# Half of a feed-forward layer's products rewritten as seven half-size products, with their sums shared out over three engines

## The chip, the cores and the metric

The kernel runs on one core of a Trainium2 chip. TensorE (PE in the profile) multiplies, VectorE (DVE) and ScalarE (ACT) read the results from PSUM, GpSimd (POOL) issues the loads and SyncE (SP) the stores and the DMA transposes. The metric is the device time of one execution in microseconds; the number compared is the median of several runs.

## What is computed

Chunked attention, then a feed-forward layer. `q`, `k`, `v` have the shape 8 x 8 heads x 576 x 64, in chunks of 64 tokens:

```
scores = 0.125 * (q_chunk @ k_chunk^T);  attn = softmax(scores);  out = attn @ v_chunk
x = out, heads side by side                # 4608 tokens x 512
h = x @ w_in                               # 512 x 2048
g = h / (1 + exp(-beta * h))
result = g @ w_out                         # 2048 x 512, float32
```

## The kernel before

**Blocks.** The 4608 tokens are nine blocks `j` of 512 tokens (two units of 256). While block `j` goes through the first layer, block `j-1` goes through the second, and the two units `2j+2` and `2j+3` go through attention. The kernel gives the order of all instructions itself: for each block a list `items` of (position in the block from 0 to 1, tie-break, work) is sorted, and the work is emitted in that order. Every engine runs its own instructions strictly in that order, each after its waits.

**First layer.** `emit_m(j, m)` makes 128 of the 2048 features for 512 tokens: four matmuls of 128x512 (`KDM` = 4 slices of the 512 inputs) into a PSUM bank `hps`, then ScalarE's tanh into `sg`, then VectorE's gate, `(sg + 1) * hps`, into the fp16 tile `gt`. Sixteen `m` make a block. `hps` comes from a pool `ps_p` of four PSUM banks.

**Second layer.** From block 1 on it is already made as seven products in place of eight (Winograd's form of Strassen's scheme): `emit_prod(j, p, t)`, eight matmuls of 128x256 for each of `p` in (1, 2, 6, 5, 7, 3, 4) and `t` in (0, 1). `emit_sum` makes the four sums `sm[0..3]` of `gt` on VectorE, `emit_wt` the four of `w_out` once. The products accumulate in two PSUM banks, `ya` (1, 6, 7, 4) and `yb` (2, then 5, 3). Partial results are copied out by ScalarE between the products, and VectorE adds the rest.

**Attention.** For unit `u` of the later blocks: `emit_T` (two DMA transposes on SP's queue, q and k), `emit_sc` (scores, then ScalarE's exponential into `et`), `emit_pv` for the halves s = 0 and 1, `emit_norm` (VectorE: a reciprocal and a product), `emit_xt_dma` (a DMA transpose on SP's queue into `xt`, which the next block's first layer reads). Scores and both halves of the PV product share one pair of PSUM banks, the pool `ps_s` with one buffer: each of the three waits until the one before it has been read. `loads_to` issues the loads of later units on GpSimd; it is called at the end of `emit_T`. The eight PSUM banks from block 3 on: four `ps_p`, two `ps_s`, `ya`, `yb`.

Of the kernel before, what the change touches and what calls it, by code (L numbers as in the profile page):

```python
# [8 lines left out]
FP32 = mybir.dt.float32  # L9
FP16 = mybir.dt.float16  # L10
ACTF = mybir.ActivationFunctionType
ALU = mybir.AluOpType
# [3 lines left out]
def kernel(  # L16
# [18 lines left out]
    NU = NT // UNIT  # L35
    NTILE = NT // 128
    VP = 80
    NV = 16
    HF = DFF // 2
    scale = 1.0 / float(D) ** 0.5  # L40

# [8 lines left out]
    gt_p = ctx.enter_context(tc.tile_pool(name="gt", bufs=2))  # L50
    sg_p = ctx.enter_context(tc.tile_pool(name="sg", bufs=3))
    osb_p = ctx.enter_context(tc.tile_pool(name="osb", bufs=4))
    osl_p = ctx.enter_context(tc.tile_pool(name="osl", bufs=6))
    ps_p = ctx.enter_context(tc.tile_pool(name="ps_p", bufs=4, space=bass.MemoryType.PSUM))
    ps_s = ctx.enter_context(tc.tile_pool(name="ps_s", bufs=1, space=bass.MemoryType.PSUM))
    ps_x_open = tc.tile_pool(name="ps_x", bufs=1, space=bass.MemoryType.PSUM)
    ps_x = ps_x_open.__enter__()
    ps_y = []

    ident = const.tile([128, 128], FP16)  # L60
    idle = const.tile([128, 512], FP16)
    HH = H // 2
    raw0 = [const.tile([128, HH, 2, D], FP32, name=f"raw{i}") for i in range(2)]
    qk0 = [[const.tile([128, HH, 2, D], FP16, name=f"h0{i}{a}") for i in range(2)] for a in range(2)]
    qkT0 = [[const.tile([128, HH, CH, 2], FP16, name=f"t0{i}{a}") for i in range(2)] for a in range(2)]
    braw = const.tile([128, 32], FP32)
# [3 lines left out]
    vbig = big.tile([128, NV, H, VP], FP16)  # L70
    wt = [big.tile([128, 8, 256], FP16, name=f"wt{i}") for i in range(4)]
    sm = [big.tile([128, 8, 256], FP16, name=f"sm{i}") for i in range(4)]

    blocks = [(u, 2) for u in range(0, NU, 2)]
    NB = len(blocks)
# [51 lines left out]
    def loads_to(u):  # L127
        while nxt[0] <= min(u, NU - 1):
            load_unit(nxt[0])
            nxt[0] += 1  # L130
# [16 lines left out]
    def emit_T(u, which=("kT", "qT")):  # L147
        for nm in which:
            src, dst = {"kT": (k_t, kT), "qT": (q_t, qT)}[nm]
            a = src.pop(u)  # L150
            t = qt_p.tile([128, H, CH, 2], FP16, tag=nm, name=nm)
            dst[u] = t
            if u >= XU:
                nc.sync.dma_start_transpose(
                    out=t.rearrange("p h s e -> p (h s e)").rearrange("p (j t) -> p j t", t=128),
                    in_=a.rearrange("p h r d -> p (h r d)"),
                )
                continue
            nc.vector.transpose(
                out=t.rearrange("p h s e -> p (h s e)").bitcast(FP32).rearrange(  # L160
                    "p (h i r) -> p h r i", h=H, r=2),
                in_=a.rearrange("p h r d -> p (h r d)").bitcast(FP32).rearrange(
                    "p (h r i) -> p h r i", h=H, r=2),
            )
        loads_to(u + 4)

    et_t = {}
    x_t = {}
# [104 lines left out]

    def emit_xt_pe(u, s):
        xf = x16_t.pop((u, s)).rearrange("p r h d -> p (r h d)")
        xp = ps_p.tile([128, 4, 128], FP16, tag="p", name="xp")
        xt = xt_at(u, s)
        for g in range(4):
            nc.tensor.transpose(out=xp[:, g, :], in_=xf[:, g * 128:(g + 1) * 128], identity=ident)  # L279
            if u == 0 and g % 2:  # L280
                nc.scalar.copy(out=xt[:, g - 1:g + 1], in_=xp[:, g - 1:g + 1])
        if u:
            nc.scalar.copy(out=xt, in_=xp)  # L283
# [4 lines left out]

    gt_t = {}

    def emit_m(j, m, c0=0, n=None):
        n = blocks[j][1] * UNIT if n is None else n
        if j not in gt_t:
            gt_t[j] = gt_p.tile([128, KFF, 512], FP16, tag="gt", name="gt")
        hps = ps_p.tile([128, 512], FP32, tag="p", name="hps")
        xr = xt_t[j].rearrange("p t (r k) (c q) -> p (t r) (k c) q", r=2, c=2)
        for kk in range(KDM):
            nc.tensor.matmul(  # L298
                out=hps[:, 0:n],
                lhsT=w_in16[m // 2][:, kk, (m % 2) * 128:(m % 2) * 128 + 128],  # L300
                rhs=xr[:, c0 // CH:(c0 + n) // CH, 2 * (kk % 2) + kk // 2, :],
                start=(kk == 0),
                stop=(kk == KDM - 1),
            )
        sg = sg_p.tile([128, 512], FP32, tag="sg", name="sg")
        nc.scalar.activation(out=sg[:, 0:n], in_=hps[:, 0:n], func=ACTF.Tanh, scale=bt[:, m:m + 1])  # L306
        nc.vector.scalar_tensor_tensor(  # L307
            out=gt_t[j][:, m, c0:c0 + n], in0=sg[:, 0:n], scalar=1.0, in1=hps[:, 0:n],
            op0=ALU.add, op1=ALU.mult,
        )  # L310
# [3 lines left out]
    def emit_t(j, t, k0=0, k1=None):  # L314
        k1 = KFF if k1 is None else k1
        if k0 == 0:
            ops_t[j, t] = ps_p.tile([128, DM], FP32, tag="p", name="ops")
        ops = ops_t[j, t]
        for kk in range(k0, k1):
            nc.tensor.matmul(  # L320
                out=ops,
                lhsT=gt_t[j][:, kk, t * 128:(t + 1) * 128],
                rhs=w_out16[kk // 4][:, kk % 4, :],
                start=(kk == 0),
                stop=(kk == KFF - 1),
            )
        if k1 < KFF:
            return
        osb = osb_p.tile([128, DM], FP32, tag="osb", name="osb")
        nc.scalar.copy(out=osb, in_=ops)  # L330
        r0 = blocks[j][0] * UNIT + t * 128
        nc.sync.dma_start(out=out[r0:r0 + 128, :], in_=osb)
# [19 lines left out]
    def emit_sum(j, i, lo=0, hi=8):  # L352
        g = gt_t[j]
        s1, s2 = sm[0][:, lo:hi, :], sm[1][:, lo:hi, :]
        a11, a12 = g[:, lo:hi, 0:256], g[:, 8 + lo:8 + hi, 0:256]
        a21, a22 = g[:, lo:hi, 256:512], g[:, 8 + lo:8 + hi, 256:512]
        a, b, op = ((a21, a22, ALU.add), (s1, a11, ALU.subtract),
                    (a11, a21, ALU.subtract), (a12, s2, ALU.subtract))[i]
        nc.vector.tensor_tensor(out=sm[i][:, lo:hi, :], in0=a, in1=b, op=op)  # L359

    acc_t = {}
    oq_t = {}
# [19 lines left out]
    def emit_prod(j, p, t):  # L382
        last = j == NB - 1
        if p == 1 and t == 0:
            if j == 1:
                a = [ps_p.tile([128, 512], FP32, tag="p", name="acc") for _ in range(2)]
            else:
                a = [ps_y[0].tile([128, 512], FP32, tag=n, name=n) for n in ("ya", "yb")]
            if last:
                a = [(a[i], ps_p.tile([128, 512], FP32, tag="p", name="acc")) for i in range(2)]  # L390
            acc_t[j] = a
        g = gt_t[j]
        acc = acc_t[j][0 if p in (1, 6, 7, 4) else 1]
# [33 lines left out]
                     7: (1, 1, "add"), 3: (0, 1, "add"), 4: (1, 0, "copy")}[p]  # L427
        key = (j, r, c, t if last else None)
        if how == "copy":
            o = osl_p.tile([128, 256], FP32, name="osl") if last else osb_p.tile([128, DM], FP32, tag="osb", name="osb")  # L430
            oq_t[key] = o
            nc.scalar.copy(out=o, in_=acc)  # L432
        else:
            o = oq_t[key]
            nc.vector.tensor_tensor(out=o, in0=acc, in1=o, op=ALU.add)
# [1 line left out]
            late.append(key)  # L437

    def emit_idle(n, w):
        d = ps_p.tile([128, 512], FP32, tag="p", name="warm")  # L440
        for _ in range(n):
            nc.tensor.matmul(out=d[:, 0:w], lhsT=idle[:, 0:128], rhs=idle[:, 0:w])

    with tc.manual_schedule():
# [93 lines left out]
        def att_items(u, a0, w):  # L538
            if u >= XU:
                return [(a0, 2, ("sc", u)), (a0 + 0.34 * w, 3, ("pv", u, 0)),  # L540
                        (a0 + 0.35 * w, 3, ("norm", u, 0)), (a0 + 0.60 * w, 3, ("pv", u, 1)),
                        (a0 + 0.61 * w, 3, ("norm", u, 1)), (a0 + 0.10 * w, 3, ("T", u + 1))]
            return [(a0, 2, ("sc", u)), (a0 + 0.40 * w, 3, ("pv", u)),
                    (a0 + 0.41 * w, 3, ("norm", u, 0)), (a0 + 0.55 * w, 3, ("norm", u, 1)),
                    (a0 + (0.70 if u + 1 < XU else 0.10) * w, 3, ("T", u + 1))]

        for j in range(1, NB):
            if j == 3:
                ps_x_open.__exit__(None, None, None)
                ps_y.append(ctx.enter_context(tc.tile_pool(name="ps_y", bufs=1, space=bass.MemoryType.PSUM)))  # L550
            items = []
            if j == 1:
# [3 lines left out]
                          (0.80, 3, ("norm", 4, 1)), (0.74, 3, ("Th", 5, "kT")), (0.86, 3, ("Th", 5, "qT"))]  # L556
            else:
                m0 = 0.36 if j == 2 else 0.02
                items += [(m0 + (1 - m0) * m / KFF, 0, ("m", m)) for m in range(KFF)]
                for i, p in enumerate((1, 2, 6, 5, 7, 3, 4)):  # L560
                    for t in range(2):
                        items.append((0.98 * (2 * i + t) / 14, 1, ("prod", p, t)))
                if j == NB - 1:
                    for i, c in ((2, 0.74), (0, 0.82), (1, 0.86), (3, 0.90)):
                        items.append((c, 4, ("pre", i)))
                for i in range(4):
                    s0 = (0.01, 0.08, 0.25, 0.33)[i] if j == 2 else 0.005 + 0.07 * i
# [12 lines left out]
            for _, _, it in items:  # L580
                if it[0] == "m":
                    emit_m(j, it[1])
                elif it[0] == "h":
                    emit_m(j, it[1], 256, 256)
                elif it[0] == "prod":
# [55 lines left out]
```

## Time and profile before

| quantity | value |
|---|---|
| median of three runs (lowest to highest) | 288.31 us (288.10 to 288.41) |
| the profiled execution's own time | 289.32 us |
| its span, first to last instruction | 287.5 us, granted TensorE clock 0.992 |
| PE / DVE / ACT / POOL busy | 95% / 68% / 51% / 34% of the span |
| blocks 3 to 7, first matmul to first matmul | 28.4 us each |
| block 8, and the second layer of block 8 with the last stores | 26.0 us and 15.8 us |

The profiled execution takes 1.0 us more than the median of the runs; 1.8 us of its time lie outside its span. "Busy" counts overlapping instructions of an engine once. In rows of instruction groups the form is given as output<-inputs (partitions x elements, type), then count, total busy us, mean ns of one, and the idle time of the engine ahead of it with what ended it.

### The profile page before, as it was taken

The page shows a single profiled execution, that of the slowest core. Times are in us where ns is not written, and L with a number is a line of the kernel's source. Part 1 is how long each engine was busy: PE and PEld are TensorE (multiplying, and loading weights), DVE is VectorE, ACT ScalarE, POOL GpSimd, SP SyncE. Part 2 cuts the span into 40 slices and gives each one's busy share as a digit, 9 for nine tenths or more (in the row PEclk, how much of TensorE's full clock was granted, in tenths as well). Part 3 has the DMA queues.
Part 4 walks back from the last instruction along what each step waited for, and adds up shares of the span by engine and source line. Part 5 has one row for each costly group of instructions (what it writes and reads, how often), then busy time and mean ns, then how long its engine had stood idle before and what let it go on. Part 6 is the DMA issues. An engine that isn't in the chain of part 4 may idle for free.

```text
span 287.5 us, 7407 instructions
## 1 busy us (share of the span) xinstructions
PE 272.6 (95%) x3090; PEld 175.7 (61%) x3090; DVE 195.6 (68%) x327; ACT 147.9 (51%) x235; POOL 97.0 (34%) x124
## 2 busy tenths in 40 slices
PE   7769999796999999999999999999999999999995
PEld 3555445653856566666666666666666666666684
DVE  3557538789577768576858685868576857685841
ACT  2368406884356464646463646364536454545521
POOL 8854578486474923434090707000000000000000
PEclk9999999999899999999999999999999999999999
DMA  9999999999999998999999998990748123110213
GB/s 138 171 196 204 174 172 187 232 167 130 109 98 150 141 214 118 149 130 193 119 105 161 178 145 105 129 228 18 112 96 144 22 55 95 53 39 31 70 48 109
DMA packets 145952, 36.92 MB, mean 128 GB/s; under 512 B 130048, under 2 KB 145408, under 8 KB 145920
## 3 DMA queue, kind: packets, MB, share of 16 engines
q0 software_dynamic: 101216, 18.10, 82.3%
q1 hardware_dynamic: 44704, 18.37, 34.8%
q8 instruction: 24, 0.39, 0.5%
q14 instruction: 8, 0.07, 0.1%
HBM read 36.71 MB, written 9.44 MB: 160 GB/s over the span
## 4 chain that ended last, share of the span: by engine, by line
PE 84%; DVE 5%; DMA 3%; POOL 3%; ACT 3%; issue 1%; DVEq 0%; ACTq 0%; POOLq 0%
PE hps L298 40%; PE ya L415 16%; PE yb L415 12%; PE acc L415 5%; PE ops L320 5%; DMA win<-in_moe_w_in_dram 3%; PE x L248 2%; DVE gt L307 2%; PE sc L227 1%; PE sc L214 1%; POOL vbig L115 1%; ACT sg L306 1%; DVE x L263 1%; ACT xt L283 1%; PE xp L279 1%
## 5 line engine op out<-in xcount | busy, mean ns | idle before, releaser
L306 ACT ACTIVATE sg<-hps,bt 128x512 f32<-128x512 f32 (+1 forms) x158 | 101.7, 650 | 94.6 <-PE hps L298 92.8
L298 PE MATMUL hps<-xt,win 128*128 128x512 f16 (+1 forms) x632 | 143.1, 360 | 2.7 <-ACT xt L283 1.3
L307 DVE SCALAR_TENSOR_TENSOR gt<-sg,hps 128x512 f16<-128x512 f32 (+1 forms) x158 | 99.7, 637 | 62.5 <-ACT sg L306 62.0
L298 PEld LDWEIGHTS <-win 128*128 128x128 f16 x632 | 59.7, 98 | 44.5 <-issue 2.6
L415 PEld LDWEIGHTS <-sm 128*128 128x128 f16 x512 | 49.2, 98 | 15.1
L415 PEld LDWEIGHTS <-gt 128*128 128x128 f16 x384 | 37.6, 100 | 12.1
L101 POOL DMA_DIRECT2D qu<-in_q_dram x22 | 18.6, 854 | 62.7 <-DMA qT<-qu 50.0
L115 POOL DMA_DIRECT2D vbig<-in_v_dram x40 | 34.2, 879 | 10.2 <-DMA wout<-in_moe_w_out_dram 4.3
L415 PE MATMUL ya<-wt,sm 128*128 128x256 f16 x208 | 27.0, 273 | 0.0
L263 DVE TENSOR_TENSOR x<-x,rd 128x512 f16<-128x512 f32 (+1 forms) x40 | 25.2, 637 | 1.2
L359 DVE TENSOR_TENSOR sm<-gt 128x2048 f16<-128x2048 f16 (+1 forms) x17 | 19.7, 1159 | 0.3
L101 POOL DMA_DIRECT2D ku<-in_k_dram x22 | 18.8, 877 | 0.0
L236 ACT ACTIVATE et<-sc 128x1024 f16<-128x1024 f32 (+1 forms) x9 | 7.3, 833 | 14.0 <-PE sc L227 13.9
L320 PE MATMUL ops<-wout,gt 128*128 128x512 f16 x64 | 14.5, 379 | 0.0
L259 DVE RECIPROCAL rd<-x 128x8 f32<-128x8 f32 x36 | 7.2, 201 | 9.9 <-PE x L248 9.9
L415 PE MATMUL ya<-wout,gt 128*128 128x256 f16 x104 | 13.5, 273 | 0.0
L415 PE MATMUL yb<-wt,sm 128*128 128x256 f16 x104 | 13.5, 273 | 0.0
L415 PE MATMUL ya<-wt,gt 128*128 128x256 f16 x104 | 13.5, 273 | 0.0
L415 PE MATMUL yb<-wout,sm 128*128 128x256 f16 x104 | 13.5, 273 | 0.0
L415 PE MATMUL yb<-wout,gt 128*128 128x256 f16 x104 | 13.5, 273 | 0.0
L248 PEld LDWEIGHTS <-et 64*64 64x64 f16 x576 | 7.2, 108 | 9.7 <-issue 6.4
L432 ACT COPY osb<-ya 128x512 f32<-128x512 f32 x18 | 10.5, 586 | 2.4 <-PE ya L415 2.4
(59 smaller groups left out, 193.0 us busy)
## 6 DMA issues: line engine op xcount, KB each, us to landing
out_dram<-osb SPq DMA_DIRECT2D x32, 256.0 KB, 4.5
vbig<-in_v_dram POOLq DMA_DIRECT2D x32, 128.0 KB, 7.4
qu<-in_q_dram POOLq DMA_DIRECT2D x20, 128.0 KB, 5.3
ku<-in_k_dram POOLq DMA_DIRECT2D x20, 128.0 KB, 6.4
win<-in_moe_w_in_dram POOLq DMA_DIRECT2D x8, 256.0 KB, 9.6
wout<-in_moe_w_out_dram POOLq DMA_DIRECT2D x4, 512.0 KB, 12.2
qu<-in_q_dram POOLq DMA_DIRECT2D x4, 256.0 KB, 7.0
ku<-in_k_dram POOLq DMA_DIRECT2D x4, 256.0 KB, 7.5
```

What stands on the lines that cost most here:

```text
L101: nc.gpsimd.dma_start(out=tv[off:off + n, sp], in_=src[b, :, s:s + n, :].rearrange("h p d -> p h d"),)
L115: nc.gpsimd.dma_start(out=vbig[off:off + n, i % NV, :, 0:D], in_=v[b, :, s:s + n, :].rearrange("h p d -> p h d"),)
L236: nc.scalar.activation(out=et[:, s], in_=sc[:, s], func=ACTF.Exp, scale=scale)
L248: nc.tensor.matmul(out=x[64 * c:64 * c + 64, r, g, 0:D + 1], lhsT=(et[64 * r:64 * r + 64, s, 4 * c + g, :] if u < XU else et[64 * r:64 * r ...
L263: nc.vector.tensor_tensor(out=o, in0=x[:, r, :, 0:D], in1=rd[:, r].to_broadcast(list(o.shape)), op=ALU.mult)
L298: nc.tensor.matmul(out=hps[:, 0:n], lhsT=w_in16[m // 2][:, kk, (m % 2) * 128:(m % 2) * 128 + 128], rhs=xr[:, c0 // CH:(c0 + n) // CH, 2 * ...
L306: nc.scalar.activation(out=sg[:, 0:n], in_=hps[:, 0:n], func=ACTF.Tanh, scale=bt[:, m:m + 1])
L307: nc.vector.scalar_tensor_tensor(out=gt_t[j][:, m, c0:c0 + n], in0=sg[:, 0:n], scalar=1.0, in1=hps[:, 0:n], op0=ALU.add, op1=ALU.mult,)
L320: nc.tensor.matmul(out=ops, lhsT=gt_t[j][:, kk, t * 128:(t + 1) * 128], rhs=w_out16[kk // 4][:, kk % 4, :], start=(kk == 0), stop=(kk == K ...
L359: nc.vector.tensor_tensor(out=sm[i][:, lo:hi, :], in0=a, in1=b, op=op)
L415: nc.tensor.matmul(out=dst, lhsT=lhsT, rhs=rhs, start=(p in (1, 2, 5) and kk == 0 and (t == 0 or last)), stop=(kk == 7 and (t == 1 or last ...
L432: nc.scalar.copy(out=o, in_=acc)
```

## The change

From block `QB` = 3 on, the features of the pairs `QM` = (2, 3), which are `m` = 8 to 15, are no longer made by `emit_m`. A pair `i` holds 512 features in two weight tiles `a = w_in16[2i]`, `b = w_in16[2i+1]`; with the 512 inputs and the 512 tokens cut in halves, it is a 2x2 block product made as seven products of half size in each direction (`emit_q_prod`, four matmuls of 128x256 each).

- Weight sums `ws` are made once for each pair on VectorE (in blocks 2 and 3). The sums of x, `tx[0..3]`, are made once for each block: on VectorE in block 3, on GpSimd from block 4 on.
- The products accumulate in two banks `qx` (1, 6, 7, 4) and `qz` (2, then 5, 3). ScalarE makes three copies for each pair, VectorE three adds. Three of the four results then lie in SBUF (`hc`), one in PSUM.
- Tanh and gate of these results go in pieces of two groups of 128 features by 256 tokens (`emit_q_late`, `emit_q_gate`). All gates stay on VectorE.
- One of the second layer's four sums, `sm[2]`, is made on GpSimd during blocks 3 to 8 (`SE`); only that of block 8's own `gt`, at the end, stays on VectorE.
- PSUM: from block 3 on two banks for `hps` (`ps_r`) in place of four, and `qx`, `qz`.
- Order: the first `m` comes at position 0.0 (was 0.02), the second layer's products 0.03 later; gates are emitted apart from their matmuls (`mg`); loads of later units get an item of their own (`ld`), a quarter of a block after the transposes they belong to.
- SBUF: `vbig` keeps 12 tiles of v in place of 16, `raw0` and the last block's output tiles share `hc_p`.

```
-    NV = 16
+    NV = 12
...
+    QM = (2, 3)
+    QB = 3
+    ws = {i: [big.tile([128, 2, 256], FP16, name=f"ws{i}{n}") for n in range(4)] for i in QM}
+    tx = [big.tile([128, 2, 4, CH], FP16, name=f"tx{n}") for n in range(4)]
...
-        nc.vector.tensor_tensor(out=sm[i][:, lo:hi, :], in0=a, in1=b, op=op)
+        eng = nc.gpsimd if i in SE and QB <= j + 1 < NB else nc.vector
+        eng.tensor_tensor(out=sm[i][:, lo:hi, :], in0=a, in1=b, op=op)
...
+    def emit_tx(j, n):
+        xq = xt_t[j].rearrange("p t (r k) (c q) -> p k c (t r) q", r=2, c=2)
+        b11, b12, b21, b22 = (xq[:, :, c, 4 * r:4 * r + 4, :] for c in range(2) for r in range(2))
+        in0, in1 = ((b12, b11), (b22, tx[0]), (b22, b12), (b21, tx[1]))[n]
+        eng = nc.vector if j == QB else nc.gpsimd
+        eng.tensor_tensor(out=tx[n], in0=in0, in1=in1, op=ALU.subtract)
...
+    def emit_q(j, i, s):
+        if s == 0:
+            qz_t[j, i] = [ps_q[0].tile([128, 512], FP32, tag=n, name=n) for n in ("qx", "qz")]
+        st = qz_t[j, i]
+        x, z = st[0:2]
+        for p in ((2, 1), (6, 5), (7, 3), (4,))[s]:
+            emit_q_prod(j, i, p)
+            if p == 2:
+                continue
+            if p in (1, 6, 5):
+                o = hc_p.tile([128, 512], FP32, tag="hc", name="hc")
+                nc.scalar.copy(out=o, in_=z if p == 5 else x)
+                st.append(o)
+            if p in (1, 7, 3):
+                o = st[{1: 2, 7: 4, 3: 3}[p]]
+                nc.vector.tensor_tensor(out=o, in0=x if p == 7 else z, in1=o, op=ALU.add)
...
+    def emit_q_late(j, i, s):
+        for r, c, h in ([(0, 0, st[2])], [], [(1, 1, 4), (0, 1, 3)], [(1, 0, st[0])])[s]:
+            q_tanh(j, i, r, c, st[h] if isinstance(h, int) else h)
...
+        SE = (2,)
+        QP = (0.08, 0.19, 0.30, 0.40, 0.55, 0.66, 0.77, 0.87)
+        QL = (0.06, 0.16, 0.26, 0.35, 0.47, 0.57, 0.67, 0.76)
+        MP0, DT, DG = 0.0, 0.04, 0.03
+        TP = (0.0, 0.001, 0.10, 0.15)
...
+                    for m in range(nm):
+                        items += [(MP0 + ml * m / nm, 0, ("mp", m)), (MP0 + ml * m / nm + DG, 3, ("mg", m))]
+                    for nq, (i, s) in enumerate((i, s) for i in QM for s in range(4)):
+                        c = (QL if j == NB - 1 else QP)[nq]
+                        items += [(c, 1, ("q", i, s)), (c + DT, 1, ("ql", i, s)), (c + DT + DG, 3, ("qg", i, s))]
+                    items += [(c, 5, ("tx", n)) for n, c in enumerate(TP)]
```

## The prediction, made before the changed kernel ran

> **What bounds the kernel now.** I read the page's chain first, then busy time by stretch cut at the blocks' first second-layer matmul, then the groups by form, then time lines of single engines.
>
> ```profile
> PE 84%; DVE 5%; DMA 3%; POOL 3%; ACT 3%; issue 1%; DVEq 0%; ACTq 0%; POOLq 0%
> ```
> ```profile
> core 0: us, PE busy (x) PEld busy (x) DVE busy (x) ACT busy (x) POOL busy (x), PEclk, DMA share, GB/s
> 160.42:188.84 28.42, 28.42 (x305) 18.25 (x304) 20.18 (x31) 14.94 (x22) 8.88 (x11) 1.00 1.66 143
> 245.70:271.74 26.04, 26.04 (x178) 17.21 (x177) 19.17 (x27) 13.34 (x20) 0.00 (x0) 1.00 0.12 41
> ```
> In blocks 3 to 8 (103.6 to 271.7 us) PE has no idle time, at full clock: a matmul less there is time less, and a wait on PE there is time more. VectorE is busy for 20.2 of 28.4 us, GpSimd only with issuing loads, until block 5. What a matmul costs is read from the chain in order of time (start, us):
>
> ```profile
> 187.27 0.87 PE ya L415 x8
> 188.14 0.86 PE hps L298 x4
> ```
> Four matmuls of 512 columns take 0.865 us, eight of 256 take 0.87: the price goes by columns, and the smaller weight loads (98 ns each) hide.
>
> **What it removes.** For a pair of block `j`, 16 matmuls of 512 (4 x 0.865 = 3.46 us) become 28 of 256 (3.5 x 0.87 = 3.05): 0.415 us less. Twelve pairs: **5.0 us less**, all of it on PE's path if PE stays fed. A block becomes 27.6 us.
>
> **What it adds, off PE.** Rows for the prices:
>
> ```profile
> L306 ACT ACTIVATE sg<-hps,bt 128x256 f32<-128x256 f32 x28 | 12.4, 476 | 3.6 <-PE hps L298 3.4
> L307 DVE SCALAR_TENSOR_TENSOR gt<-sg,hps 128x512 f16<-128x512 f32 x130 | 88.3, 684 | 56.6 <-ACT sg L306 56.4
> L359 DVE TENSOR_TENSOR sm<-gt 128x2048 f16<-128x2048 f16 x15 | 18.3, 1222 | 0.2
> L435 DVE TENSOR_TENSOR osb<-yb,osb 128x512 f32<-128x512 f32 x12 | 8.2, 684 | 0.0
> ```
> Back to back they start closer than they last, as VectorE's time line shows (start, us): a sum takes 1.13, a reciprocal 0.24, a normalization or gate 0.61.
>
> ```profile
> 139.21 1.22 DVE L359 TENSOR_TENSOR sm<-gt 128x2048 f16<-128x2048 f16 x1
> 140.34 0.20 DVE L259 RECIPROCAL rd<-x 128x8 f32<-128x8 f32 x1
> 140.58 0.69 DVE L263 TENSOR_TENSOR x<-x,rd 128x512 f16<-128x512 f32 x1
> 141.19 0.68 DVE L307 SCALAR_TENSOR_TENSOR gt<-sg,hps 128x512 f16<-128x512 f32 x1
> ```
> VectorE gets six adds (3.6 us), keeps sixteen gates, loses one sum (1.1): 22.7 of 27.6 us. ScalarE gets six copies (0.59 each) and sixteen tanhs of 256 (0.48) for eight of 512 (0.69): 15 + 3.5 + 2.2 = 21 us at most. Both fit on average; what counts is when. From the order of the built kernel's instructions I walk one block, its first matmul at 0, a result readable 0.2 us after its last matmul:
>
> - The last gate of the block before ends at 1.3 (its product ends at -1.7, two tanhs, 0.6). Then `sm[0]` to 2.4, gate `m` = 0 to 3.0, `sm[1]` to 4.1, first add to 4.7, its tanhs on ScalarE to 5.65, its gate to 6.3, gate `m` = 1 to 7.0, reciprocal and norm of the first half to 7.85.
> - PE's order: product 5, which overwrites the bank the first add reads, is due at 6.5; the second half's PV, which needs the norm's bank, at 8.65. Both are met, by 1.8 and 0.8 us. Later margins: 0.2 us (product 1 of the second pair after the gate from PSUM), 0.45 (its product 4 after the adds). So with undisturbed engines a block costs PE nothing, but **VectorE's lateness has under a microsecond of cover** in the first third.
>
> Smaller costs, each once: (a) In block 3 `ya` lies in a bank that was `hps`; its first product comes 0.87 us after the last `m` of block 2, whose tanh and gate take 0.2 + 0.7 + 0.7: 0 to 0.9, I take 0.4. (b) `xt`: the last transpose of the five blocks lands 2.4 to 5.5 us after its issue, and is now issued at 22.6 in a block that needs it at 27.6; only block 5's 5.5 is too long: 0 to 1.5, I take 0.6.
>
> ```profile
> xt<-x SPq DMA_TRANSPOSE x1, 5.5
> ```
> (c) In block 5 `tx` is queued on GpSimd behind unit 16's loads, which in the run before end 3.6 us after that block's start (shown: their first and last groups); with a block shorter by 0.8 us `tx[1]` comes at 6.2 for product 6 at 6.0: 0 to 1.5, I take 0.3. In the other blocks the loads end by the first microsecond; the transposes on SP's queue keep their places.
>
> ```profile
> 158.77 1.76 POOL L101 DMA_DIRECT2D qu<-in_q_dram  x2 [8.36 <-DMA qT<-qu]
> 162.25 1.79 POOL L115 DMA_DIRECT2D vbig<-in_v_dram  x2
> ```
> (d) At the end VectorE has `sm` halves, a last gate and all of `sm[2]` ahead of the upper half of `sm[1]`: that is ready 7.5 us after the last product of layer one, product 6 wants it at 6.5: 0 to 1.5, I take 0.9. Sum 2.2. The weight sums (eight of 128x512; 2048 columns take 1.22 us and 1024 0.69, so 512 some 0.42) hide in blocks 2 and 3, where VectorE idles 7 us; bare, they would cost 3. Twelve tiles of v in place of sixteen cost nothing: GpSimd's loads wait 50 us in total for `qT`, none for a tile of v.
>
> **What no row shows: GpSimd computing beside VectorE.** The nearest rows of its own price are its only operation that reads SBUF and a memset of one column:
>
> ```profile
> 9.19 0.29 POOL masks.py:199 TENSOR_SCALAR_AFFINE_SELECT ident<-ident 128x128 f16<-128x128 f16 x1
> 0.24 0.10 POOL L625 MEMSET const-float32-0.0<- 128x1 f32 x1 [0.24 <-issue]
> ```
> 0.19 us for 128 columns gives 0.86 for a `tx` (512) and 3.1 for `sm[2]` (2048). Bounds: VectorE's own 0.42 and 1.2 below, twice the estimate above, for two inputs in place of one (1.6 and 6.2). I take 0.86 and 3.1.
>
> The second unknown is whether VectorE's instructions with both inputs in SBUF (sums, and the gates of copied results) wait while GpSimd reads SBUF. Lower bound: not at all, as VectorE's sums run 1.22 us with or without GpSimd's load issues beside them. Upper bound: for the whole GpSimd instruction. The row for the lower bound is not near, since an issue reads no tensor; I take the upper one, as GpSimd's 6.5 us (3.1 and four times 0.86) then come just where VectorE's margin is smallest. Walked: `sm[2]` can start at 0.4 and runs to 3.5; `sm[0]`, ready at 1.3, goes 3.5 to 4.65; gate 0 to 5.25; `tx[3]` takes its turn, `sm[1]` 5.5 to 6.65; first add to 7.25, so product 5 starts 0.9 late; gate of that result at 8.8, gate 1 at 9.4, norm to 10.3, so PV starts another 0.85 late. **1.7 us in each of blocks 4 to 7, 6.8**; in block 8, which has no PV, product 5 comes 1.2 late; block 3, where `sm[2]` runs at the block's start and `tx` is on VectorE, has room. 8.0 us. With the doubled price each block loses some 3 us more: about +15.
>
> [...]
>
> **Sum.** -5.0 + 2.2 + 8.0 = +5.2 us on the profiled execution's 289.3, which stands 1.0 above the median of the runs: 288.3 + 5.2, **293.5**.
>
> **Rivals.**
> - *The two engines run side by side* (VectorE's lower bound). Then -5.0 + 2.2 = -2.8: **285.5**, between 283.3 (no small cost) and 287.5. For it: PE's gap-free blocks and the prices by column, which are rows, not guesses. Against: VectorE's margins of 0.2 to 0.8 us. It decides as long as VectorE's delay in the first third of a block stays under 0.8 us; beyond that each microsecond counts five times.
> - *Transposes late.* DMA is busy 9 tenths until 190 us; if blocks shortened by 0.8 us only make `xt` late in blocks 3 to 5 (1 to 1.5 us each), 3.5 of the gain go: **288 to 289**. Against it: from block 6 on DMA is mostly under half busy, and the last landings take 2.4 us.
> - *The products don't take 0.87.* Four matmuls to a weight sum, not eight, change weights as often; if a switch of bank cost 0.1 us (as after the 64x64 matmuls, 0.98 for 0.87), 7 x 0.1 eats each pair's 0.415: **291**. Against it: in the chain `hps` and `ya` alternate at 0.86 and 0.87.
>
> **How the numbers follow.** Waiting engines 0.52 (289 to 302 with the price of GpSimd); side by side 0.38; late transposes 0.06; dearer products 0.04. A measurement of this kernel tells 0.2% from no change. Faster by more: nearly all of the second case, and a little of the third, 0.39. Slower by more: the first, the fourth and a part of the third, 0.56. Within: 0.05. The range must hold both signs: 284.2 leaves out a tenth of all below, 300 a tenth above. The likeliest case alone: 289.5 to 300.
>
> **What the profile after would show.** Right: products `qx`, `qz` at 0.435 for four; PE idle in blocks 4 to 7 by 1 to 4 us each, put down to VectorE ahead of product 5 and the second PV; `sm` and `gt` instructions on VectorE that last 2 us or more while GpSimd runs `sm[2]`. Wrong: sums and gates at 1.22 and 0.69 throughout and blocks of 27.6 us. A GpSimd `sm[2]` far from 3.1 us mis-sizes it either way.

## The result, and the profile after

The changed kernel takes **311.38 us** (309.26 to 313.31) beside 288.36 for the kernel before on the same chip: ratio 1.0787, 95% interval 1.0691 to 1.0883, so 23 us slower, where the prediction had 293.5 and 300.0 as its upper end. The direction and the mechanism of the likeliest case were right; its size was not. The profiled run took 313.04 us, its span is 311.3.

The page first, its busy tenths of the span, PE's granted clock and the chain of waits:

```profile
PE   6699998969999599996999799969996999599995
PEclk9989999999999899999899999998999999869999
PE 48%; DVE 29%; ACT 9%; issue 7%; DMA 4%; POOL 2%; ACTq 0%; DVEq 0%; POOLq 0%
```

PE was 84% of the chain and VectorE 5%; now VectorE (DVE) is 29%. PE has a hole in every block from 3 on, and behind some of these holes its granted clock falls to half (0.50 from 209 to 212 us, in block 6), where the kernel before has 1.00 over its blocks 3 to 8. Cut at the first matmul of each block, blocks 3 to 8 read (columns as in the prediction's second fence; the 28.42-us block there is what to compare, 26.04 for the last one):

```profile
101.95:134.98 33.03, 29.49 (x328) 21.27 (x328) 28.75 (x47) 18.70 (x37) 13.06 (x13) 0.95 1.38 139
...
167.84:198.55 30.71, 27.89 (x328) 20.48 (x328) 26.12 (x35) 17.93 (x35) 18.38 (x13) 1.00 1.05 130
198.55:231.05 32.50, 29.57 (x330) 21.09 (x328) 27.57 (x37) 18.47 (x37) 10.51 (x6) 0.95 0.39 82
...
263.06:294.99 31.93, 28.55 (x203) 20.68 (x201) 25.02 (x31) 17.29 (x36) 8.06 (x4) 0.89 0.09 30
```

What PE waited for (total us, times, longest), the three new ones:

```profile
PE qz L432 <- DVE hc L456: 8.8, 3, 3.1
PE x L257 <- DVE x L272: 6.3, 3, 2.8
PE ya L521 <- DVE gt L327: 3.0, 1, 3.0
```

Product 5 behind the first add, the second half's PV behind the norm, and block 3's first second-layer product behind the last gate of block 2. Now the groups, to be held against VectorE's sum of 1222 ns and gate of 684 before:

```profile
L405 DVE SCALAR_TENSOR_TENSOR gt<-sq,hc 128x512 f16<-128x512 f32 x36 | 34.2, 952 | 9.1 <-ACT sq L414 7.8
L304 DVE SCALAR_TENSOR_TENSOR gt<-sg,hps 128x512 f16<-128x512 f32 x48 | 32.7, 680 | 10.7 <-ACT sg L323 10.7
L380 DVE TENSOR_TENSOR sm<-gt 128x2048 f16<-128x2048 f16 x9 | 23.6, 2622 | 0.0
L380 POOL TENSOR_TENSOR sm<-gt 128x2048 f16<-128x2048 f16 x6 | 24.4, 4067 | 0.0
```

VectorE's gates of a result in PSUM (`hps`) cost what they did; gates of a copied result (`hc`, both inputs in SBUF) and sums grew, though their shapes are the same. GpSimd (POOL) needs 4.07 us for a `sm[2]`. The time line of block 6 shows the two meeting (start, us):

```profile
198.85 1.60 POOL L395 TENSOR_TENSOR tx<-xt 128x512 f16<-128x512 f16 x1
200.41 4.06 POOL L380 TENSOR_TENSOR sm<-gt 128x2048 f16<-128x2048 f16 x1
200.55 5.00 DVE L380 TENSOR_TENSOR sm<-gt 128x2048 f16<-128x2048 f16 x1
205.48 0.67 DVE L304 SCALAR_TENSOR_TENSOR gt<-sg,hps 128x512 f16<-128x512 f32 x1
206.08 1.57 DVE L380 TENSOR_TENSOR sm<-sm,gt 128x2048 f16<-128x2048 f16 x1
207.57 0.68 DVE L456 TENSOR_TENSOR hc<-qz,hc 128x512 f32<-128x512 f32 x1
208.30 0.60 PE L432 MATMUL qz<-tx,ws 128*128 128x256 f16 x4 [2.87 <-DVE hc L456]
208.73 1.77 PE L521 MATMUL yb<-wout,gt 128*128 128x256 f16 x8
```

VectorE's `sm[0]` comes 0.14 us after GpSimd's `sm[2]`, stands until that ends, and lasts 5.00 us; everything queued behind it shifts, and product 5 comes 2.87 us late. The last row is the second loss: eight matmuls that last 1.04 us elsewhere take 1.77, at a granted clock of 0.75 from 208.75 and 0.50 from 209.00 us on.

**The balance** (spans). Blocks 3 to 8 take 193.0 us in place of 168.2. With gap-free products they would take some 163.7 (the last experiment's 27.68 in five, 26.04 less a like 0.75 in the last). Of the 29.3 us above that, the waits that the time line lists for PE in these blocks sum to 19.8; the clock, one less its mean in each row above times its length (1.65, 1.6, 1.6 and 3.5), is 8.4 at most, as the end of block 8's wait lies in a stretch at half clock; some 1.1 us are left for waits too short to be listed.

### The profile page after: what moved, and what is told of

It is laid out like the page before. It is cut to its first block, busy times and chain, and to the rows that moved or that the text cites. A ratio compares the mean times of both kernels' runs of the same rounds, so it can differ in the third digit from the quotient of the medians.

```text
span 311.3 us, 7846 instructions
## 1 busy us (share of the span) xinstructions
PE 275.9 (89%) x3234; PEld 190.9 (61%) x3234; DVE 240.0 (77%) x369; ACT 169.9 (55%) x319; POOL 153.9 (49%) x150
## 4 chain that ended last, share of the span: by engine, by line
PE 48%; DVE 29%; ACT 9%; issue 7%; DMA 4%; POOL 2%; ACTq 0%; DVEq 0%; POOLq 0%
PE hps L315 17%; DVE sm L380 10%; PE yb L521 6%; PE ya L521 6%; DVE gt L405 5%; ACT sq L414 4%; PE ops L340 4%; DVE gt L304 4%; DMA ku<-in_k_dram 4%; PE qx L432 4%; PE qz L432 3%; PE acc L521 3%; DVE gt L327 3%; ACT sg L323 3%; DVE hc L456 2%
## 5 line engine op out<-in xcount | busy, mean ns | idle before, releaser
L315 PE MATMUL hps<-xt,win 128*128 128x512 f16 (+1 forms) x440 | 98.3, 362 | 2.9 <-DMA xt<-x 1.3
L323 ACT ACTIVATE sg<-hps,bt 128x512 f32<-128x512 f32 (+1 forms) x110 | 68.5, 630 | 35.5 <-PE hps L315 34.1
L315 PEld LDWEIGHTS <-win 128*128 128x128 f16 x440 | 42.4, 100 | 33.0 <-issue 5.4
L414 ACT ACTIVATE sq<-hc,bt 128x256 f32<-128x256 f32 x72 | 31.4, 498 | 49.8 <-DVE hc L456 49.8
L521 PEld LDWEIGHTS <-sm 128*128 128x128 f16 x512 | 49.9, 99 | 10.5 <-DVE sm L380 0.6
L521 PEld LDWEIGHTS <-gt 128*128 128x128 f16 x384 | 38.6, 101 | 12.8 <-issue 4.9
L327 DVE SCALAR_TENSOR_TENSOR gt<-sg,hps 128x512 f16<-128x512 f32 (+1 forms) x62 | 34.3, 562 | 13.3 <-ACT sg L323 12.9
L405 DVE SCALAR_TENSOR_TENSOR gt<-sq,hc 128x512 f16<-128x512 f32 x36 | 34.2, 952 | 9.1 <-ACT sq L414 7.8
L304 DVE SCALAR_TENSOR_TENSOR gt<-sg,hps 128x512 f16<-128x512 f32 x48 | 32.7, 680 | 10.7 <-ACT sg L323 10.7
L432 PEld LDWEIGHTS <-ws 128*128 128x128 f16 x192 | 18.2, 99 | 14.4 <-issue 9.3
L521 PE MATMUL ya<-wt,sm 128*128 128x256 f16 x192 | 25.8, 279 | 0.0
L380 DVE TENSOR_TENSOR sm<-gt 128x2048 f16<-128x2048 f16 (+1 forms) x11 | 24.9, 2270 | 0.0
L380 POOL TENSOR_TENSOR sm<-gt 128x2048 f16<-128x2048 f16 x6 | 24.4, 4067 | 0.0
L395 POOL TENSOR_TENSOR tx<-xt,tx 128x512 f16<-128x512 f16 x10 | 18.2, 1820 | 0.4
```

The lines of the kernel that those rows point to most:

```text
L304: nc.vector.scalar_tensor_tensor(out=gt_t[j][:, m, :], in0=sg, scalar=1.0, in1=hps, op0=ALU.add, op1=ALU.mult,)
L315: nc.tensor.matmul(out=hps[:, 0:n], lhsT=w_in16[m // 2][:, kk, (m % 2) * 128:(m % 2) * 128 + 128], rhs=xr[:, c0 // CH:(c0 + n) // CH, 2 * ...
L327: nc.vector.scalar_tensor_tensor(out=gt_t[j][:, m, c0:c0 + n], in0=sg[:, 0:n], scalar=1.0, in1=hps[:, 0:n], op0=ALU.add, op1=ALU.mult,)
L380: eng.tensor_tensor(out=sm[i][:, lo:hi, :], in0=a, in1=b, op=op)
L395: eng.tensor_tensor(out=tx[n], in0=in0, in1=in1, op=ALU.subtract)
L405: nc.vector.scalar_tensor_tensor(out=gt_t[j][:, m:m + 2, 256 * c:256 * c + 256], in0=sv, scalar=1.0, in1=hv, op0=ALU.add, op1=ALU.mult,)
```

## The experiments

Each ran beside the kernel before on its chip; the ratio is to that. Where no long wait stands ahead of it, block 3's first second-layer product still started anywhere from 102.1 us (number 10) to 105.1 us (number 12); so where a microsecond counts, block lengths are compared and not medians alone. Lengths are from a block's first matmul to the next block's.

**1. `sm[2]` back on VectorE.**
```
-        SE = (2,)
+        SE = ()
```


> As the changed kernel, but all four sums of the second layer are on VectorE again; GpSimd keeps only the sums of x (tx). Theory (VectorE's instructions with two SBUF inputs wait for the whole GpSimd instruction that reads SBUF): the 4.0 to 5.0 us sums and gates vanish, none lasts over about 3 us; the 3 us waits of PE in blocks 3 to 8 and the half-clock stretches behind them go, VectorE has 1.1 us more to do per block; 291 to 298 us. Rival (VectorE is simply overfull, or its order is too tight, and GpSimd's help is needed): blocks get longer than the 32 us of the changed kernel, 311 us or more.

293.56 us (291.88 to 294.56), ratio 1.0199 [1.014, 1.0259]. One sum per block moved back gives 17.8 of the 23 us. No half clock is left in the blocks: from 100 to 280 us the granted clock is 1.00. `tx` on GpSimd still stretches VectorE: gates of copied results average 866 ns, sums 1492, and the second PV waits 4.1 us in four times.

**2. Nothing computed on GpSimd.** `SE = ()`, and in `emit_tx`:
```
-        eng = nc.vector if j == QB else nc.gpsimd
+        eng = nc.vector
```


> As the changed kernel, but GpSimd computes nothing: sm[2] and all tx on VectorE. Theory: every sum lasts 1.22 us and every gate 0.69 again, PE's waits shrink to what VectorE's longer queue leaves (about 1 to 2 us a block at the second PV), no half clock in blocks 4 to 8; 286 to 292 us. Rival (VectorE overfull): 24.5 of 27.6 us busy is too much, blocks of 30 us or more, 300 us and above. Rival (products of 256 columns cost more than by columns): four matmuls of qx or qz take over 0.47 us back to back.

290.98 us (289.66 to 292.76), ratio 1.0109 [1.0069, 1.0149]: with `tx` off GpSimd too, another 2.6 us are back. Sums have their old mean again, and so have gates of copied results (689 ns):

```profile
L380 DVE TENSOR_TENSOR sm<-gt 128x2048 f16<-128x2048 f16 x15 | 18.3, 1219 | 0.0
```

VectorE now does all the added work, and the kernel is still 3 us slower than before: blocks 4 to 7 take 28.68 us, 1.0 more than number 12's. PE waits there in short pieces, each given as the time line lists it and as the starts of the matmuls show it: PV behind the norm 0.40 and 0.46 us, product 1 of the second pair behind a gate 0.17 and 0.34, a block's first second-layer product behind a copy on ScalarE 0.07 and 0.24.

**3. `sm[2]` alone on GpSimd.** The second kernel with `SE = (2,)`.

> As the changed kernel, but tx is on VectorE in every block and only sm[2] is on GpSimd. Theory: one instruction of VectorE in each block still lasts 4 us or more, PE still waits some 2 to 3 us in each block and drops to half clock behind it: 302 to 311 us, nearer to the changed kernel than the kernel without sm[2] on GpSimd is. Rival (the many short GpSimd instructions, not the long one, do the harm): below 296 us.

310.39 us (309.55 to 312.72), ratio 1.0781 [1.0719, 1.0842]. The whole loss is back with six instructions. What VectorE has next to GpSimd's sum is now a `tx`, and its group shows it (0.42 us undisturbed):

```profile
L395 DVE TENSOR_TENSOR tx<-xt 128x512 f16<-128x512 f16 x12 | 22.4, 1868 | 0.0
```

**4. The kernel before, with `sm[2]` of blocks 3 to 8 on GpSimd.**
```
-        nc.vector.tensor_tensor(out=sm[i][:, lo:hi, :], in0=a, in1=b, op=op)
+        eng = nc.gpsimd if i == 2 and 3 <= j + 1 < NB else nc.vector
+        eng.tensor_tensor(out=sm[i][:, lo:hi, :], in0=a, in1=b, op=op)
```


> The kernel before with one edit: sm[2] on GpSimd in blocks 3 to 8. No seven products in the first layer. Theory: in each of the six blocks one VectorE instruction with two SBUF inputs (the next sum) lasts up to 5 us in place of 1.22, the gates behind it are late, PE waits for hps or the norm 1 to 3 us in each block although VectorE's total work falls by 1.1 us a block; 292 to 305 us. Rival (the harm needs the seven products' fuller queues; with VectorE at 20 of 28.4 us there is room): 287 to 289 us.

304.06 us (302.6 to 305.75), ratio 1.0572 [1.0505, 1.064]. The number fits the theory, the cause only in part. The waits of PE say

```profile
PE ya L416 <- POOL sm L360: 7.3, 2, 5.5
PE sc L214 <- issue: 2.9, 1, 2.9
```

In blocks 3 to 5 GpSimd's queue holds the loads, which wait for `qT`; the sum stood behind them, and twice it was late for its own product (7.3 us). The 2.9 us, which this view gives to no engine ("issue"), are in block 5 and end just after a norm that stood behind this sum of VectorE, the one place where the theory's own case came up:

```profile
179.85 6.50 DVE L360 TENSOR_TENSOR sm<-gt,sm 128x2048 f16<-128x2048 f16 x1
```

Blocks 6 to 8, whose 4.08-us sums no load held up, lost nothing. So most of this run's loss is GpSimd's lateness, not what was disputed; number 10 leaves the lateness out.

**5. GpSimd busy with writes only.** The second kernel, and at the place of `sm[2]`:
```
...
+    nc.gpsimd.tensor_tensor(out=idle[:, 0:1], in0=g[:, 7, 0:1], in1=g[:, 6, 0:1], op=ALU.subtract)
+    for _ in range(5):
+        nc.gpsimd.memset(idle, 0.0)
```


> The kernel of the second experiment (every sum, every tx and every gate on VectorE, 290.98 us) with GpSimd kept busy at the place of sm[2] in blocks 3 to 8: one operation on a single column of gt (it fixes the time at which it may start), and then five memsets of a 128x512 f16 tile that nothing reads, some 4 us in all, as long as sm[2] was. GpSimd so writes SBUF for as long, but reads next to none of it. Theory (VectorE's two-SBUF-input instructions wait for a GpSimd instruction that has SBUF inputs): sums stay at 1.22 and gates at 0.69 us mean, no half clock inside the blocks, and the time stays at 290 to 293 us. Rival (any GpSimd instruction that works on SBUF makes them wait): VectorE instructions of up to 4 us beside the memsets and 297 to 311 us.

290.52 us (289.77 to 292.46), ratio 1.008 [1.005, 1.011], the same as the second kernel. The groups:

```profile
L739 POOL MEMSET idle<- 128x512 f16 x30 | 15.8, 525 | 1.7
L380 DVE TENSOR_TENSOR sm<-gt 128x2048 f16<-128x2048 f16 x15 | 18.3, 1218 | 0.0
```

Five memsets are 2.6 us of SBUF writes in a block, not the 4 intended. Gates of copied results don't fall beside them, but sums and `tx` do: five of the sums run beside memsets for 0.83 to 1.11 us and last 1.22 each, and ten `tx` keep their 0.42. So VectorE didn't wait for GpSimd's writes; in number 3, where its `tx` takes 1868 ns in place of the 418 here, GpSimd's instruction also reads two inputs.

**6. `sm[2]` alone on GpSimd, in four pieces.**
```
+            for h in range(0, 8, 2):
+                eng.tensor_tensor(out=sm[i][:, h:h + 2, :], in0=a[:, h:h + 2], in1=b[:, h:h + 2], op=op)
```


> The kernel of the third experiment (sm[2] alone on GpSimd, 310.39 us) with GpSimd's sm[2] as four instructions of 512 columns in place of one of 2048. Theory (a waiting VectorE instruction waits for one whole GpSimd instruction, then gets its turn): no single wait on VectorE beyond about 1.2 us, the sum of waits in a block smaller, since VectorE comes between the pieces, no half clock in blocks 4 to 8, and 293 to 301 us. Rival (what counts is GpSimd's total time, four waits one after the other where there was one): 306 to 311 us, with PE waits still near 3 us and half clock as in the third experiment.

297.6 us (296.02 to 298.17), ratio 1.0291 [1.0253, 1.0329], 12.8 less than with one piece:

```profile
L382 POOL TENSOR_TENSOR sm<-gt 128x512 f16<-128x512 f16 x24 | 29.3, 1262 | 63.5 <-PE ya L525 49.6
L399 DVE TENSOR_TENSOR tx<-xt 128x512 f16<-128x512 f16 x12 | 8.5, 707 | 0.0
```

GpSimd reads longer in all (4 x 1.26 = 5.0 us for 4.07), yet VectorE's `tx` falls from 1868 to 707 ns: from block 4's sum on no VectorE instruction stands for more than one piece of 1.26 us, so there GpSimd kept VectorE out for an instruction, not for the whole sum. No half clock came in blocks 4 to 8 (granted clock 1.00 in each); PE's longest wait there is 1.1 us. Block 3 is otherwise: a weight sum of 0.42 us stood through three pieces, and a wait of PE of 2.29 us, with half clock behind it (0.50 from 107.5 us on), remains.

```profile
101.79 4.77 POOL L382 TENSOR_TENSOR sm<-gt 128x512 f16<-128x512 f16 x4
102.32 3.23 DVE L392 TENSOR_TENSOR ws<-win,ws 128x512 f16<-128x512 f16 x1
```

So that a waiting instruction gets its turn after one piece isn't shown for every case. And shorter instructions may not be the whole gain: for blocks 6 to 8 three of the four pieces began some 7 us ahead of the block, as their inputs were ready, and there held up no VectorE instruction. No run tells the two apart.

**7. VectorE's order.** The second kernel, the sums and two `tx` moved out of the first third of a block:
```
-        TP = (0.0, 0.001, 0.10, 0.15)
+        TP = (0.0, 0.001, 0.19, 0.26)
-    ... 0.005 + 0.07 * i
+    ... (0.005, 0.075, 0.43, 0.48)[i]
```


> The kernel of the second experiment with VectorE's order moved: the sums of blocks 3 to 8 at 0.005, 0.075, 0.43 and 0.48 of a block in place of 0.005, 0.075, 0.145 and 0.215, and tx[2], tx[3] at 0.19 and 0.26 in place of 0.10 and 0.15, so that gates and the norm in the first third of a block no longer stand behind sm[2], sm[3], tx[2] and tx[3]. Theory (what the second experiment still lost, 0.9 us a block, is VectorE's order and no price of the products): blocks of 27.6 to 27.9 us, waits on PE within blocks 4 to 7 below 0.3 us each, and 285 to 287.5 us. Rival (the seven products cost more than 0.435 us for four, or later instructions of the block move into PE's way): blocks stay at 28.3 or more and 289 to 292 us.

287.45 us (286.25 to 289.26), ratio 0.9968 [0.9941, 0.9995]. Blocks 4 to 7 take 28.07: between theory and rival. The starts of matmuls show two small waits that are left in each: product 1 of the second pair 0.21 us behind the gate that `sm[2]` now stands before, and a block's first second-layer product 0.24 us behind a copy on ScalarE.

**8. The tail.** As 7, and the last block's `sm[2]` behind the upper halves of `sm[0]` and `sm[1]`.

> The kernel with VectorE's order moved, and at the end of the kernel the whole of sm[2] made behind the upper halves of sm[0] and sm[1] in place of ahead of them. Theory (term (d) of the prediction: the upper half of sm[1] comes late for product 6 of the last block because sm[2] is ahead of it): 0.3 to 0.9 us less than without this. Rival (product 4's tail is bound by something else, the last gate or the copies out): within 0.2 us of it, or sm[2] itself late for its own product and 0.3 us more.

286.1 us (285.53 to 287.62), ratio 0.9922 [0.9893, 0.9952]. The one wait on `sm` in the tail (0.32 us) is gone; from the first product of the last second layer to its product 4 it takes 10.57 us in place of 10.97. So 0.4 us are shown; the rest of the difference to 7 is spread.

**9. Three small moves.** As 8, sums 2 and 3 at 0.475 and 0.53, the scores ahead of a block's first second-layer product, `tx[3]` of block 8 at 0.22.

> The kernel with VectorE's order and the tail moved (286.1 us), and three small moves more, aimed at the waits that its blocks of 28.07 us still hold: sums 2 and 3 at 0.475 and 0.53 in place of 0.43 and 0.48 (product 1 of the second pair waited 0.2 us for a gate behind sm[2]), the scores ahead of a block's first second-layer product (that product waited 0.24 us for a copy on ScalarE), tx[3] of block 8 at 0.22 (its product 4 waited 0.3 us). Theory (the seven products and the rest of a block cost 27.6 us on PE, as predicted, and what is above it is waits): blocks 4 to 7 of 27.6 to 27.75 us and 283.5 to 285.5 us. Rival (28.07 is what the products cost with their bank and weight switches): blocks stay within 0.1 of 28.07 and 285.7 to 287 us.

287.37 us (285.38 to 288.63), ratio 0.9973 [0.9943, 1.0003]; blocks of 28.2. A miss: the waits aimed at are gone, but `sm[2]` was now late for its own product 7 (`ya L521 <- DVE sm L380`, five times 0.29 to 0.35 us in the waits, 0.52 by the starts).

**10. The kernel before, with `sm[2]` of blocks 6 to 8 on GpSimd** (number 4 with `6 <= j + 1`).

> The kernel before with sm[2] on GpSimd in blocks 6 to 8 alone, where no load stands ahead of it on GpSimd's queue. Every gate and norm of this kernel has an input in PSUM; only the sums have two in SBUF. Theory (the two engines exclude each other only where the VectorE instruction has both inputs in SBUF): gates and norms stay at 0.69 us beside sm[2]'s 4.1, blocks 6 to 8 stay PE-bound at 28.4, and the time is within 0.3% of the kernel before. Rival (GpSimd's work slows VectorE or PE in general): 2 to 3 us more in each of three blocks, 294 to 298 us.

287.5 us (286.5 to 290.37), ratio 1.0 [0.9968, 1.0033]. Blocks 6 to 8 take 28.42, 28.43 and 26.04 us, as before, and so does block 5 with 28.43: GpSimd, idle, took up each sum 8.8 us ahead of the block that it was ordered in (at 178.63, 207.10 and 235.53 us). GpSimd's row, and VectorE's gates in the same stretch:

```profile
L360 POOL TENSOR_TENSOR sm<-gt 128x2048 f16<-128x2048 f16 x3 | 12.2, 4066 | 53.6 <-PE ya L416 53.6
```
```profile
L307 DVE SCALAR_TENSOR_TENSOR gt<-sg,hps 128x512 f16<-128x512 f32 x50 | 34.3, 685 | 27.4 <-ACT sg L306 27.4
```

With the same 4.07-us sum beside them, gates that read PSUM stay at 685 ns. Where these three sums ran, VectorE had nothing but gates, norms and adds with an input in PSUM, and GpSimd's sum was free; in the changed kernel it was not: there VectorE's sums and gates of copied results, both inputs in SBUF, stand beside it, 2622 and 952 ns on the mean.

**11. The order of 9, with GpSimd's part put back.** `SE = (2,)`, `tx` of blocks 4 to 8 on GpSimd.

> The same small moves with GpSimd's part of the change put back: sm[2] on GpSimd in blocks 3 to 8 and tx in blocks 4 to 8. Theory (what costs is VectorE standing still for some 4 us of a block while sm[2] reads, wherever it is put, since every 4 us of a block hold a gate of a copied result or a sum that PE needs soon): VectorE instructions of 2 to 5 us, PE waits of 1 to 3 us in each block, 293 to 308 us. Rival (only the old place, ahead of the first third's gates, was bad, and later there is room): blocks of 27.6 to 28 us and 284 to 287 us, since VectorE has less to do.

310.26 us (307.82 to 317.08), ratio 1.0771 [1.0682, 1.086]: as the theory expected. In blocks 3 to 5, where loads stand ahead of it on GpSimd's queue, `sm[2]` did come later, 14.5, 13.3 and 11.8 us into the block, and PE waited 4.74, 3.25 and 1.66 us behind gates of copied results. The rival falls there. Block 4:

```profile
148.16 5.22 DVE L405 SCALAR_TENSOR_TENSOR gt<-sq,hc 128x512 f16<-128x512 f32 x1 [0.44 <-ACT sq L414]
148.68 4.15 POOL L380 TENSOR_TENSOR sm<-gt 128x2048 f16<-128x2048 f16 x1
```

In blocks 6 to 8 nothing held it up, and a later place in the order didn't hold back an idle engine: in block 6 `sm[2]` still started 3.5 us into the block, as soon as GpSimd was through with `tx`.

```profile
200.26 5.03 POOL L380 TENSOR_TENSOR sm<-gt 128x2048 f16<-128x2048 f16 x1
```

Here GpSimd's sum lasts 5.03 us in place of 4.07: VectorE's `sm[0]` had stood there since 199.30, and this time GpSimd waited. But the earlier start didn't always win: block 4's gate began 0.52 us ahead of `sm[2]` and stood through it all the same, as did a weight sum of 6.14 us in block 3 (1.74 us ahead) and number 4's sum of 6.50 us (1.29 ahead). In all three GpSimd was issuing loads just ahead of its sum. Load issues alone stretched nothing in number 2 (20 such VectorE instructions stand beside them, and its sums and gates of copied results average 1219 and 689 ns); why these three waited stays open.

**12. The blocks closed.** As 9, sum 2 at 0.365 and sum 3 at 0.48, so that sum 2 fills a time in which VectorE waits for ScalarE.

> The kernel with the three small moves, with sum 2 at 0.365 and sum 3 at 0.48 in place of 0.475 and 0.53: sum 2 then starts in the 0.44 us in which VectorE waits for ScalarE, ahead of the gates of the first pair, instead of behind the gate that product 1 of the second pair waits for (product 7 of the second layer waited 0.5 us for it there). Theory (a block's matmuls take 27.6 to 27.7 us and the rest of what was seen is waits that VectorE's order makes): blocks 4 to 7 of 27.6 to 27.75 us, no wait of PE above 0.15 us in them, and 1.5 to 2.5 us less than the kernel with the three small moves, 285 to 286. Rival (VectorE has no room for all four sums, 22.7 us of work among fixed times, and each place for sum 2 makes another wait): blocks stay at 28.0 to 28.2 us and the time at 286 to 287.5 us.

**285.76 us** (283.65 to 287.63), ratio 0.9923 [0.9887, 0.9959]: 0.8% faster than the kernel before, and over 25 us faster than the changed one. Its chain and two blocks:

```profile
PE 78%; DVE 7%; DMA 5%; ACT 4%; POOL 3%; issue 2%; ACTq 0%; DVEq 0%; POOLq 0%
```
```profile
132.88:160.56 27.68, 27.68 (x340) 20.59 (x329) 24.89 (x42) 18.47 (x37) 9.44 (x13) 1.00 1.57 154
160.56:188.24 27.68, 27.68 (x337) 20.60 (x329) 24.89 (x42) 18.46 (x37) 7.94 (x10) 1.00 1.79 159
```

PE is busy for all of 27.68 us while VectorE works 24.9 of them. Between this one and number 8 the medians don't decide (ratios 0.9923 and 0.9922, each to the kernel before on its own chip); the blocks do (27.68 and 28.07).

## Why the prediction was right or wrong

- **What is removed: right.** A block without waits takes 27.68 us (number 12) where the prediction had 27.6: 0.75 less than the 28.43 before, where 0.83 was forecast. Four matmuls of 256 start 0.44 after the four before. The rival of dearer products falls (its own terms give 288.3 - 5.0 + 8.4 = 291.7, not 291).
- **That engines exclude each other, the upper bound: right.** Before the run it was a choice between two bounds: no row of the kernel before has a GpSimd sum beside VectorE. Instructions with both inputs in SBUF waited for a GpSimd sum, which reads SBUF (number 3: `tx` of 1868 ns), and not for memsets, which only write (number 5: 418); gates that read PSUM didn't wait (680 against 952 ns in the changed kernel, 685 in number 10). The wait was for a whole instruction (the changed kernel's 4.06 and 5.00 us), in both directions (number 11's 5.03 in place of 4.07). It wasn't always the later one that waited: in three rows of numbers 4 and 11 VectorE's instruction began ahead of GpSimd's sum and stood through it all the same (6.50, 5.22 and 6.14 us), and in block 3 of number 6 VectorE stood through three instructions, not one (3.23 us). The rival of engines side by side falls with number 3 alone (310.39 us).
- **The price of it, 8.0 us: the failed step.** PE's waits for an add or a norm of VectorE in blocks 4 to 8 are 15.1 us. Three terms were mis-sized. The length: `sm[2]` lasts 4.07 us, not 3.1; the row of a 128-column operation with one input was too far from it. The start: `sm[2]` was walked from 0.4 to 3.5 us of a block; in block 6 it ran from 1.9 to 5.9, since `tx[0]`, `tx[1]` and `tx[2]` stand ahead of it on GpSimd's queue, each 1.1 us alone and up to 2.1 when it has to wait for VectorE, not 0.86. The direction: the walk took each wait of VectorE for GpSimd, and none the other way. So in block 6 product 5 came 2.87 us late, not 0.9 and then 0.85 for PV (by the walk's own times, 7.25 against 6.5 and 10.3 against 9.55, it would be 0.75 and 0.75).
- **Block 3 "has room": wrong.** `sm[2]` ran from 100.32 to 104.45, beside the last weight sum, which lasted 4.26 us in place of 0.42 and had two of block 2's gates behind it; PE waited 3.01 us. Only the first third of a block had been walked, not the end of the one before, so these 3.0 us stood at nothing.
- **PE at half clock: not in the sum at all.** Up to 8.4 us of the loss. The steps took a wait to cost its own length and no more. With the 7.1 us that blocks 4 to 8 wait above the 8.0 and block 3's 3.0, that is 18.5, about the 17.9 by which the result lies above 293.5.
- **Small costs.** (a) Block 3's handover is 0.6 us without GpSimd (number 2), 0.4 expected. (b) `xt` was late in three blocks (0.24, 0.53, 0.49), not in block 5 alone: 1.3 us against 0.6. (c) Loads didn't hold up `tx` in block 5: they had ended 2.5 us before `tx[0]` began, at the block's start, when the late `xt` had landed. In blocks 4 and 5 `sm[2]` so came 5.6 and 5.4 us into the block; PE's wait there is for the norm behind a gate of 4.00 us, and `tx` itself wasn't waited for. (d) The tail's wait is 0.32 us, not 0.9. And a change of 0.2% can't be told here: the intervals above reach 0.3 to 1.0% either way.
- **"With undisturbed engines a block costs PE nothing": not as ordered.** Number 2 isn't quite that case, as VectorE has `sm[2]` and `tx` too, some 2.8 us in a block; it lost 1.0 us a block, 0.8 of it at the places with the small margins (second PV, product 1 of the second pair). Number 12 shows that this work fits, at zero waits, in another order. How the changed kernel's own order would run with GpSimd's part free can't be tried.

## What to carry to other kernels

Before work goes to GpSimd, list what VectorE runs beside it: here a 4.07-us sum was free beside gates that read PSUM (685 ns, number 10), and instructions with both inputs in SBUF could stand for the whole of it (5.00 us in place of 1.22 in the changed kernel), so that balance by busy time said nothing. Cut what must stay there into short instructions (12.8 us less for four pieces, some of it perhaps because three of them could start earlier), and remember that an idle queue started when inputs were ready, whatever its place in the order (8.8 us ahead of the block in number 10). With margins under a microsecond, first place VectorE's instructions into its own waits: the change was worth 2 us on VectorE alone, number 8's 0.4 in the tail included, and cost 23 with help.

## What the hardware showed that was not expected

In these traces half clock comes in stretches whose starts lie on a grid. In the changed kernel's the granted clock falls to 0.5 behind the waits of blocks 3, 4, 6 and 8, for 3.41 us each (6.83 behind block 8's); the four starts lie 40.96, 61.44 and 61.44 us apart, 12, 18 and 18 times 3.413. Two in number 3, at 145.99 and 241.57 us, lie 95.6 us apart, 28 times 3.413. It isn't the length of a wait alone that decides: in number 6 one of 2.29 us brought it, in number 11 one of 3.25 didn't. Laid on the grid of its own run, carried on in windows of 3.413 us, the first lies with 0.67 of a window within one, the second is cut by an edge into 0.47 and 0.48; block 6's 2.87 us of the changed kernel fill 0.83 of one, block 7's 2.79 us, which brought nothing, 0.49 and 0.33. Over blocks 3 to 8 of the changed kernel and numbers 3, 6 and 11, each window of which the listed waits fill 0.61 or more was followed by one at half clock. Of those filled to 0.49 or less one was: block 8's first window at half clock, filled to 0.31, was followed by a second. Two between lie too close to tell (0.54 with, 0.55 without, both number 3). In the changed kernel half clock takes up to 8.4 of 311 us. Runs of this kernel lie near 309.5 or near 313.2 us, at mean clocks of 0.976 and 0.962 to 0.967; only one of them has a trace, so what tells them apart isn't shown. All of this is read off traces; no run moves a wait against the grid alone.
